# A GEGLU feed-forward in float32r: one H tile of each pair summed in its PSUM bank, and permuted rows moved from the output stores to the loads of layer norm 2

## The chip, the cores and the metric

One Trainium2 chip, one core. The metric is device microseconds of one execution. TensorE (PE) multiplies, VectorE (DVE), ScalarE (ACT) and GpSimd (POOL) do the rest; SyncE (SP) issues nearly all DMAs, ScalarE a few.

## The reference, cut

```python
h = x + attention(layernorm(x))              # 2048 tokens x 512, 32 heads, 4 segments of 512 tokens with a memory
g = layernorm(h) @ w_gate                    # 512 x 1376
u = layernorm(h) @ w_up
out = h + (gelu_tanh(g) * u) @ w_down        # 1376 x 512
```

All is float32. The kernel splits each operand of a product into a high and a low float32r part and adds three products (high x high, high x low, low x high).

## The kernel before

The tokens are 16 tiles of 128. The feed-forward treats them in two halves, `p` = 0 and 1, of two segments `s` of four tiles `t`. The 1376 columns are 11 blocks `f` (ten of 128, one of 96), taken in the order 0, 1, 10, 2, 3 to 9 (`forder`). What is written in the functions is only recorded: `pe`, `act`, `dve`, `pool` and `dma` make a list of steps, and the numbers of `ORDER` (lines 58 to 328) say in which order `Sched.run` issues them, each to its engine's own queue. `Val` stands for a buffer, which is handed out when its first step is issued; `row` buffers (128 x 512 floats), `slot`, `stk` and `stq` (a high and a low part) lie in SBUF, the eight `bank` in PSUM. Steps of one engine run in the order of its queue; SP's DMAs use eight completion semaphores in turn (DMAHW0 to DMAHW7, shared with the DMAs that ACT issues), and one waits until the one before it on its semaphore has landed.

`ffn(p, f, b)` (lines 1551 to 1613) multiplies weights and blocks of the normed tokens in seven products for a 2x2 block scheme, sums them (L1568 copies a bank, L1573 adds), and `geglu(s, g_, u_)` makes the H tile of block f and segment s: a square on ACT (L1579), a sum (L1581), a tanh on ACT (L1583), and two products on DVE (L1586, L1588). H tiles lie in `row` buffers as HH[p, f, s].

The down product takes pairs of blocks. For the first five pairs of half 0 and the first four of half 1 (`BY7`), `down7(p, n)` (lines 1704 to 1763) again makes seven products out of the four H tiles b11, b12 (block 2n) and b21, b22 (block 2n + 1). It needs t1 = b12 - b11, t2 = b22 - t1, t3 = b22 - b12 and t4 = b21 - t2 (`sub`, L1711 on DVE), and a `split` of the seven operands: a copy on ACT (L1716) and a difference on POOL, or on DVE for t2 and t4 of three pairs of half 0 (L1718). The products (L1737) are added into eight accumulators by DVE (L1748). `wd_prep` combines the weights of the pair for it.

At the end of a half, `turned(p)` transposes the accumulators (L716), stores them in pieces to y_dram, loads rows back (L1774), and adds on POOL the rows of g_dram, where the other blocks' sums were put (L1775). In half 0 that is the output, stored by L1778. In half 1 the pair of blocks 8 and 9 is still to come: `down(1, (8, 9), ..)` multiplies on TensorE (L1628), adds on DVE (L1636) and stores the output (L1641), the second half of the last tile by ACT's queue. `split` of its H tiles is L1593 on ACT and L1596 on POOL or DVE.

The normed tokens of half 1 are stored and loaded again by blocks (`swap`, t_dram), so that row 32 a + j of tile t is token 128 a + 32 t + j of its segment. `tokens(x, p, s, t)` gives these rows of a DRAM tensor: it is used for the loads of h for the first down sums (`acc`, L1799) and for the output stores.

Of the kernel before, what the change touches and what calls it, by code (L numbers as in the profile page):

```python
# [11 lines left out]
OP = mybir.AluOpType  # L12
# [3 lines left out]
P = 128  # L16
# [42 lines left out]
    6, 2, 10, 100, 0, 1, 4, 5, 11, 9, 7, 12, 13, 27, 14, 8, 16, 76, 77, 18, 91, 92, 93, 28, 29, 30, 15, 17, 88, 89,  # L59
    31, 32, 33, 44, 87, 23, 90, 34, 24, 46, 19, 20, 94, 95, 21, 22, 35, 36, 101, 37, 102, 103, 96, 822, 104, 25, 110,  # L60
    105, 42, 43, 38, 39, 40, 41, 821, 825, 97, 98, 99, 826, 827, 26, 828, 111, 106, 112, 628, 629, 107, 113, 108, 829,
    114, 109, 118, 48, 115, 50, 3, 52, 79, 119, 128, 129, 116, 117, 120, 164, 47, 133, 165, 121, 144, 51, 82, 167,
    168, 169, 145, 135, 146, 134, 147, 45, 139, 824, 130, 123, 124, 49, 53, 138, 81, 830, 54, 55, 831, 75, 131, 132,
    136, 58, 137, 140, 122, 186, 166, 189, 151, 149, 150, 148, 181, 184, 183, 185, 253, 254, 59, 74, 127, 190, 188,
    182, 57, 126, 187, 176, 178, 1024, 255, 823, 56, 173, 179, 175, 256, 125, 257, 180, 174, 177, 832, 833, 834, 60,
    61, 634, 1028, 835, 836, 67, 68, 258, 170, 171, 62, 172, 191, 192, 65, 66, 63, 64, 69, 70, 71, 259, 260, 72, 73,
    143, 142, 141, 197, 199, 162, 161, 198, 193, 194, 195, 196, 261, 270, 272, 271, 157, 277, 262, 263, 78, 266, 265,
    275, 152, 153, 264, 85, 273, 154, 837, 438, 439, 213, 216, 274, 217, 214, 215, 276, 440, 631, 224, 225, 226, 86,
    227, 228, 441, 278, 442, 239, 242, 243, 240, 1029, 203, 206, 205, 207, 234, 237, 443, 83, 238, 241, 235, 280, 268,
    1026, 204, 208, 209, 210, 211, 84, 163, 444, 229, 230, 279, 231, 212, 232, 233, 236, 200, 445, 245, 248, 838, 246,  # L70
    247, 201, 202, 218, 219, 446, 448, 449, 1027, 447, 839, 302, 303, 306, 450, 297, 299, 249, 244, 840, 80, 300, 632,
    220, 222, 221, 301, 1030, 298, 223, 304, 1414, 633, 281, 282, 841, 305, 155, 156, 842, 630, 250, 251, 283, 292,
    295, 294, 293, 1031, 406, 843, 296, 286, 287, 407, 635, 636, 328, 331, 332, 408, 844, 288, 845, 318, 329, 319,
    846, 847, 848, 320, 409, 410, 849, 321, 289, 313, 290, 291, 307, 308, 330, 269, 267, 366, 369, 368, 370, 314, 315,
    316, 317, 411, 323, 326, 324, 361, 365, 367, 364, 363, 362, 322, 412, 309, 413, 1025, 1032, 353, 355, 354, 158,
    625, 310, 311, 312, 626, 627, 414, 427, 429, 325, 334, 335, 336, 337, 797, 428, 433, 432, 356, 358, 357, 360, 437,
    434, 359, 798, 799, 430, 431, 415, 416, 421, 377, 380, 1033, 387, 388, 390, 800, 420, 801, 1034, 350, 352, 351,
    327, 333, 417, 378, 418, 338, 159, 1035, 284, 419, 391, 371, 339, 160, 340, 285, 372, 373, 374, 375, 392, 395,
    802, 382, 393, 394, 383, 384, 803, 398, 385, 386, 422, 482, 486, 485, 483, 804, 399, 1036, 466, 468, 401, 805,
    808, 484, 467, 807, 806, 809, 852, 586, 402, 477, 480, 1037, 481, 478, 381, 587, 376, 479, 503, 506, 379, 504,  # L80
    389, 514, 423, 588, 507, 396, 517, 469, 470, 515, 851, 505, 589, 472, 473, 518, 498, 499, 500, 501, 502, 590,
    1038, 1039, 397, 493, 496, 471, 474, 475, 508, 341, 511, 509, 591, 426, 476, 494, 424, 603, 425, 1417, 435, 436,
    541, 544, 542, 818, 252, 815, 592, 1040, 543, 819, 536, 538, 537, 545, 593, 539, 487, 488, 516, 489, 490, 491,
    492, 594, 595, 546, 540, 550, 596, 601, 608, 609, 610, 457, 600, 602, 458, 549, 1041, 512, 495, 510, 597, 598,
    497, 513, 547, 548, 400, 403, 404, 611, 612, 599, 519, 520, 1224, 578, 579, 580, 581, 582, 1225, 533, 535, 534,
    567, 568, 570, 571, 569, 613, 1226, 530, 532, 562, 563, 565, 531, 551, 552, 1227, 1228, 572, 614, 575, 573, 574,
    615, 662, 664, 663, 521, 617, 1042, 657, 658, 659, 405, 660, 661, 1229, 564, 604, 553, 554, 555, 1230, 649, 650,
    651, 666, 342, 665, 1231, 816, 1043, 557, 558, 559, 560, 1232, 616, 561, 566, 576, 652, 654, 656, 767, 1235, 1236,
    1418, 653, 820, 655, 556, 694, 697, 695, 1233, 344, 768, 646, 648, 647, 667, 1234, 618, 605, 606, 607, 781, 769,
    678, 681, 679, 770, 1044, 722, 771, 723, 726, 724, 343, 459, 460, 683, 686, 684, 850, 577, 583, 584, 785, 688,  # L90
    689, 1045, 1046, 1047, 1048, 1049, 685, 696, 817, 698, 725, 668, 1050, 1051, 691, 692, 1052, 772, 673, 522, 727,
    731, 729, 728, 674, 690, 773, 680, 682, 669, 730, 671, 670, 675, 676, 677, 687, 774, 672, 714, 715, 716, 775, 786,
# [1787 lines left out]
```

## Time and profile before

| | us |
|---|---|
| median of 3 runs (785.12 to 785.21) | 785.21 |
| the profiled execution | 783.71 |
| its span | 782.0 |
| TensorE busy | 726.2 |
| VectorE busy | 648.4 |
| ScalarE busy | 534.3 |
| GpSimd busy | 554.0 |

The granted TensorE clock is 0.983 of full on average. The profiled execution is 1.5 us under the median and 1.7 above its span. Start times count from the start of the span. A row of the timeline gives start, duration, engine, line, operation and tiles; a row of waits gives who waited, for whom, the sum in us, the count, the longest. "SPq" and "ACTq" are the queues that issue DMAs, and the duration there is that of the issue.

### The profile page before, as it was taken

The numbers are of one execution on the slowest core, as the hardware profiler recorded it, in microseconds if no ns is written. First come the engines' busy times: TensorE is split into PE (matmuls) and PEld (weight loads), VectorE is DVE, ScalarE is ACT, GpSimd is POOL, SyncE is SP. The second block draws the span as 40 slices with busy tenths as digits, with TensorE's granted clock in tenths as the row PEclk, the third lists the DMA queues.
The fourth block names the chain that finished last, engine by engine and source line by source line (L and its number), as shares of the span: only waits on it lengthen the run. The fifth ranks groups of instructions, "written<-read, shape, count | busy, mean of one in ns | idle before, by whom it ended". The sixth has DMA issues, their size and how long they took to land.

```text
span 782.0 us, 19221 instructions
## 1 busy us (share of the span) xinstructions
PE 726.2 (93%) x6442; PEld 569.7 (73%) x6442; DVE 648.4 (83%) x1978; ACT 534.3 (68%) x1138; POOL 554.0 (71%) x827
## 2 busy tenths in 40 slices
PE   7999999999999999999999998999999989999940
PEld 6877877777787776766777876787777768877830
DVE  7897989889887888999985667899999977889950
ACT  6879889796858778688675666787767746643500
POOL 6364342554745556888978999999999759999640
PEclk9999999999999999999999999999999999999985
DMA  6555556556567776767557466735752467665742
GB/s 242 135 154 145 136 151 188 140 162 175 157 181 180 227 200 167 220 202 189 179 157 229 136 233 188 226 126 150 219 170 102 113 200 230 208 230 184 190 122 81
DMA packets 100210, 137.32 MB, mean 176 GB/s; under 512 B 17440, under 2 KB 40144, under 8 KB 100112
## 3 DMA queue, kind: packets, MB, share of 16 engines
q1 hardware_dynamic: 99820, 135.71, 59.5%
q8 instruction: 51, 0.84, 0.5%
q10 hardware_dynamic: 292, 0.39, 0.2%
q14 instruction: 47, 0.39, 0.2%
HBM read 70.67 MB, written 39.26 MB: 141 GB/s over the span
## 4 chain that ended last, share of the span: by engine, by line
PE 22%; DVE 13%; POOL 10%; DMA 5%; issue 4%; ACT 2%; SPq 1%; POOLq 0%; DVEq 0%; ACTq 0%
PE bank L1561 12%; PE bank L1737 4%; DVE row L1748 2%; DVE row L1711 2%; POOL slot L1718 2%; POOL row L1533 2%; DMA g_dram<-row 2%; PE bank L1377 2%; PE bank L1297 1%; POOL half L1687 1%; POOL stq L1526 1%; POOL row L1775 1%; DVE bank L1573 1%; DVE row L1581 1%; POOL slot L1526 1%
## 5 line engine op out<-in xcount | busy, mean ns | idle before, releaser
L1275 ACT ACTIVATE row<-bank 128x512 f32<-128x512 f32 x320 | 171.8, 608 | 27.3 <-PE bank L1269 25.7
L1283 POOL TENSOR_SCALAR_AFFINE_SELECT row<-row 128x256 f32<-128x256 f32 (+1 forms) x320 | 108.7, 365 | 91.6 <-ACT row L1275 90.6
L1221 DVE CUSTOM_DVE_ANT_0 aside<-bank,amask 128x256 f32<-128x256 f32 (+2 forms) x384 | 141.0, 419 | 15.4 <-PE bank L1211 11.0
L957 PE MATMUL bank<-slot,slot 64*128 64x512 f32 x720 | 112.5, 404 | 0.1
L1561 PE MATMUL bank<-slot,slot 128*128 128x512 f32 (+1 forms) x354 | 95.2, 392 | 0.7 <-ACT vaug L1568 0.7
L1221 DVE CUSTOM_DVE_ANT_0 bank<-bank,amask 128x512 f32<-128x512 f32 x128 | 86.2, 710 | 8.6 <-PE bank L1211 7.8
L1269 PE MATMUL bank<-stq,stk 64*128 64x128 f32 (+3 forms) x512 | 81.7, 337 | 1.6 <-DVE bank L767 0.4
L1211 PE MATMUL bank<-stk,stq 64*128 64x512 f32 (+3 forms) x512 | 77.2, 329 | 4.0 <-DVE nm L1221 1.5
L1748 DVE TENSOR_TENSOR row<-row,bank 128x512 f32<-128x512 f32 x110 | 71.5, 675 | 10.8 <-PE bank L1737 9.4
L1297 PE MATMUL bank<-row,vaug 128*32 128x256 f32 (+3 forms) x1024 | 78.1, 436 | 1.1 <-DVE nm L1221 0.6
L1561 PEld LDWEIGHTS bank<-slot,slot 128*128 128x128 f32 (+1 forms) x354 | 65.4, 186 | 17.0 <-ACT vaug L1568 1.5
L957 PEld LDWEIGHTS bank<-slot,slot 64*128 64x128 f32 x720 | 70.8, 185 | 5.9 <-DVE tock L562 0.4
L1526 POOL TENSOR_TENSOR slot<-row,slot 128x512 fp32r<-128x512 f32 (+3 forms) x56 | 65.6, 1176 | 6.3 <-ACT slot L1524 5.7
L1211 PEld LDWEIGHTS bank<-stk,stq 64*128 64x128 f32 x512 | 53.3, 185 | 17.5 <-DVE nm L1221 2.8
L1269 PEld LDWEIGHTS bank<-stq,stk 64*128 64x128 f32 x512 | 55.3, 185 | 13.3 <-DVE nm L1221 3.5
L1737 PE MATMUL bank<-slot,half 128*128 128x512 f32 x216 | 58.2, 393 | 3.5 <-DVE row L1748 3.3
L1297 PEld LDWEIGHTS bank<-row,vaug 128*32 128x32 f32 x1024 | 29.8, 109 | 38.5 <-issue 32.9
L1006 PE MATMUL bank<-slot,slot 64*128 64x256 f32 x672 | 52.9, 284 | 0.0
L1561 PE MATMUL bank<-slot,stq 128*128 128x512 f32 (+1 forms) x180 | 50.5, 393 | 1.8 <-POOL stq L1526 1.2
L1737 PEld LDWEIGHTS bank<-slot,half 128*128 128x128 f32 x216 | 40.0, 188 | 14.0 <-DVE row L1748 5.6
L1221 DVE DVE_READ_ACCUMULATOR2_ANT nm<- 128x1 f32 x512 | 50.0, 98 | 0.0
L1006 PEld LDWEIGHTS bank<-slot,slot 64*128 64x128 f32 x672 | 47.5, 186 | 1.4 <-DVE z L1170 0.4
(225 smaller groups left out, 1779.0 us busy)
## 6 DMA issues: line engine op xcount, KB each, us to landing
stq<-slot SPq DMA_DIRECT2D x96, 128.0 KB
stk<-slot SPq DMA_DIRECT2D x94, 128.0 KB
row<-x SPq DMA_DIRECT2D x32, 256.0 KB
pv_dram<-row SPq DMA_DIRECT2D x32, 256.0 KB
row<-r_dram SPq DMA_DIRECT2D x28, 256.0 KB
wd_dram<-half SPq DMA_DIRECT2D x28, 256.0 KB
half<-wd_dram SPq DMA_DIRECT2D x28, 256.0 KB
row<-h_dram SPq DMA_DIRECT2D x24, 256.0 KB
```

What stands on the lines that cost most here:

```text
L957: return nc.tensor.matmul(pm[i].t, w[i].t[rows_of(r), wi, dc * P:(dc + 1) * P], XT[s][dc].t[rows_of(r), xi, :], start=(dc, wi, xi, ph) == ...
L1006: return nc.tensor.matmul(pms[n].t[:, 256 * t:256 * t + 256], XT[s][dc].t[rows_of(r), xi, t0:t0 + P], whl[wi].t[rows_of(r), dc // 2, 256 * ...
L1211: nc.tensor.matmul(sa.t[:, c0:c0 + w], sq.t[own, p, i * P:(i + 1) * P], sk.t[own, p, 0:w], start=True, stop=True, tile_position=(64 * a, 0 ...
L1221: nc.vector.tensor_tensor_reduce(out=(sa.t[:, c0:c0 + w] if i > 2 else aside[:, turns[0]:turns[0] + w]), in0=sa.t[:, c0:c0 + w], in1=amask ...
L1269: nc.tensor.matmul(sc.t[:, c0:c0 + D - q0], sk.t[own, p, q0:q0 + P], sq.t[own, p, q0:D], start=True, stop=True, tile_position=(64 * a, 0), ...
L1275: act(w, prio, lambda sc=sc, e=e: nc.scalar.activation(e.t[:, :w], sc.t[:, :w], AF.Exp), [sc, vtab], [e])
L1283: nc.gpsimd.affine_select(v, v, pattern=pat + [[1, P]], compare_op=OP.is_ge, fill=0.0, base=0, channel_multiplier=-1)
L1297: nc.tensor.matmul(pv.t[32 * n:32 * n + 32, kb * P:D], va.t[:, 136 * kb + 17 * j:136 * kb + 17 * j + 32], e.t[:, lo:lo + D - kb * P], star ...
L1526: pool(0.14 + 2.13e-3 * (hi - lo), prio, lambda: nc.gpsimd.tensor_tensor(v.t[:, 1, :hi - lo], r.t[:, lo:hi], v.t[:, 0, :hi - lo].bitcast(F ...
L1561: nc.tensor.matmul(dst.t[:w], v.t[:, wi, c0 + j * w:c0 + (j + 1) * w], b[bk][j].t[:, xi, :], start=first and j == 0 and n == 0, stop=j == ...
L1737: nc.tensor.matmul(dst[u].t, ws[a].t[0][:, wi, P * u:P * u + P], h[bk].t[:, xi], start=first and m == 0, stop=m == 2, skip_group_check=True)
L1748: dve(D, prio, lambda u=u, acc=acc: nc.vector.tensor_tensor(acc.t, acc.t, src[u].t, op=OP.add), [src[u]], [acc])
```

## The change

In `geglu` the last product of segment 1 of the odd block of a pair is written over the bank of g (`o = g_`), and this bank is HH[p, f, 1]. `down7` takes the odd block as b11, b12, so that b12 is the tile in the bank (`wd_prep` swaps the weights to fit); t3 is made first into a row, then t1 and after it t2 in the bank, then t4 into a row. The splits of t1 and t2 read the bank and are made by ACT and DVE, the other five of all pairs by ACT and POOL. `tokens` gives plain rows in both halves. Layer norm 2 of half 1 loads its rows in the permuted order instead, each tile by four loads of 32 rows, and its blocks are then in the plain order. ORDER is new throughout (2 lines of it longer).

```diff
-    6, 2, 10, 100, 0, 1, 4, 5, 11, 9, 7, 12, 13, 27, 14, 8, 16, 76, 77, 18, 91, 92, 93, 28, 29, 30, 15, 17, 88, 89,
...
+    5282, 5283,
@@ -1585,9 +1587,10 @@
             r = g_ if s else e
             dve(D, prio, lambda: nc.vector.scalar_tensor_tensor(
                 r.t[:w], e.t[:w], 1.0, g_.t[:w], op0=OP.add, op1=OP.mult), [g_, e], [r])
+            o = g_ if s and f % 2 and by7(p, f) else e
             dve(D, prio, lambda: nc.vector.scalar_tensor_tensor(
-                e.t[:w], r.t[:w], 0.5, u_.t[:w], op0=OP.mult, op1=OP.mult), [u_, r], [e])
-            HH[p, f, s] = hh or e
+                o.t[:w], r.t[:w], 0.5, u_.t[:w], op0=OP.mult, op1=OP.mult), [u_] if o is r else [u_, r], [o])
+            HH[p, f, s] = hh or o
             if not hh:
                 return
             act(D, prio, lambda: nc.scalar.activation(hh.t[:w, 0], e.t[:w], AF.Copy), [e], [hh],
@@ -1643,10 +1646,7 @@
 
     def tokens(x, p, s, t, cs=slice(0, D)):
         r0 = (8 * p + 4 * s) * P
-        if p == 0:
-            return x[r0 + t * P:r0 + t * P + P, cs]
-        return bass.AP(tensor=x.tensor, offset=x.offset + (r0 + 32 * t) * D + cs.start,
-                       ap=[[P * D, 4], [D, 32], [1, cs.stop - cs.start]])
+        return x[r0 + t * P:r0 + t * P + P, cs]
 
     vhalf = Val()
 
@@ -1665,7 +1665,7 @@
     def wd_prep(n):
         prio = at(0, 2 * n) - 12
         raw = [Val(PRAW), Val(PRAW)]
-        for r, f in zip(raw, (2 * n, 2 * n + 1)):
+        for r, f in zip(raw, (2 * n + 1, 2 * n)):
             dma(prio, lambda r=r, f=f: nc.sync.dma_start(r.t, wdp[f * P:f * P + P]), [], [r])
 
         def half(v, k):
@@ -1704,30 +1704,30 @@
     def down7(p, n):
         prio = at(p, 2 * n + 1) + 0.9
         ws = WDV[p, n]
-        b11, b12, b21, b22 = [HH[p, 2 * n + i, s] for i in range(2) for s in range(2)]
-        t1, t2 = Val(PC), Val(PC)
+        (b11, b12), (b21, b22) = [[HH[p, 2 * n + i, s] for s in range(2)] for i in (1, 0)]
+        t3, t4 = Val(PC), Val(PC)
 
         def sub(d, a, c):
             dve(D, prio, lambda: nc.vector.tensor_tensor(d.t, a.t, c.t, op=OP.subtract),
                 [v for v in (a, c) if v is not d], [d])
 
-        def split(v, on=pool):
-            hh = Val(PHH)
-            act(D, prio, lambda: nc.scalar.activation(hh.t[:, 0], v.t, AF.Copy), [v], [hh], src=0.09)
-            eng = nc.gpsimd if on is pool else nc.vector
-            on(1.23 if on is pool else D, prio, lambda: eng.tensor_tensor(
+        def split(v):
+            hh, psum = Val(PHH), v is b12
+            act(D, prio, lambda: nc.scalar.activation(hh.t[:, 0], v.t, AF.Copy), [v], [hh], src=0.067 if psum else 0.09)
+            eng = nc.vector if psum else nc.gpsimd
+            (dve if psum else pool)(D if psum else 1.23, prio, lambda: eng.tensor_tensor(
                 hh.t[:, 1], v.t, hh.t[:, 0].bitcast(F32), op=OP.subtract), [v], [hh])
             return hh
-        sub(t1, b12, b11)
-        h = {"11": split(b11), "t1": split(t1)}
-        sub(t2, b22, t1)
-        h["t2"] = split(t2, dve if p == 0 and n < 3 else pool)
-        h["21"] = split(b21)
+        h = {"11": split(b11), "21": split(b21)}
+        sub(t3, b22, b12)
+        sub(b12, b12, b11)
+        h["t1"] = split(b12)
+        h["t3"] = split(t3)
         sub(b12, b22, b12)
-        h["t3"] = split(b12)
+        h["t2"] = split(b12)
         h["22"] = split(b22)
-        sub(t2, b21, t2)
-        h["t4"] = split(t2, dve if p == 0 and n < 3 else pool)
+        sub(t4, b21, b12)
+        h["t4"] = split(t4)
         X, Y, Z = [[Val(PD) for _ in range(2)] for _ in range(3)]
 
         def prod(a, bk, dst, first=False):
@@ -1797,7 +1797,7 @@
             s, t = divmod(i, 4)
             n = 8 * p + 4 * s
             dma(at(p, 0) - 2 + i / 4, lambda i=i, s=s, t=t: nc.sync.dma_start(
-                a[i].t, tokens(h_dram, p, s, t)), HD[n:n + 4] if p else [HD[n + t]], [a[i]])
+                a[i].t, tokens(h_dram, p, s, t)), [HD[n + t]], [a[i]])
         return a
     halves()
     for p in range(2):
@@ -1815,9 +1815,11 @@
                     prio = at(0, 8) + s
                     rows = [Val(PROW2 if s else PROW) for _ in range(4)]
                     for t in range(4):
-                        r0 = (8 + 4 * s + t) * P
-                        dma(prio - 8, lambda t=t, r0=r0, rows=rows: nc.sync.dma_start(
-                            rows[t].t, h_dram[r0:r0 + P]), [HD[8 + 4 * s + t]], [rows[t]])
+                        for a in range(4):
+                            r0 = (8 + 4 * s + a) * P + 32 * t
+                            dma(prio - 8, lambda t=t, r0=r0, rows=rows, a=a: nc.sync.dma_start(
+                                rows[t].t[32 * a:32 * a + 32], h_dram[r0:r0 + 32]),
+                                [HD[8 + 4 * s + a]], [rows[t]], kb=70, dur=0.5, chain=True)
                     ln2(B[1], rows, s, prio, True, PD, swap=t_dram[s])
             if k < 22:
                 ffn_weights(*todo[k])
```

VectorE at a pair of half 1 (blocks 4 and 5). Before, with sums and differences in rows:

```order
L1586 SCALAR_TENSOR_TENSOR bank_66<-row_130,bank_66 128x512
L1588 SCALAR_TENSOR_TENSOR row_130<-bank_66,vaug_144 128x512
L1711 TENSOR_TENSOR row_118<-row_130,row_112 128x512
L1588 SCALAR_TENSOR_TENSOR row_133<-row_133,bank_65 128x512
L1748 TENSOR_TENSOR row_104<-row_104,bank_68 128x512
L1573 TENSOR_TENSOR bank_69<-vaug_142,bank_69 128x512
L1748 TENSOR_TENSOR row_115<-row_115,bank_66 128x512
L1711 TENSOR_TENSOR row_130<-row_113,row_130 128x512
L1711 TENSOR_TENSOR row_125<-row_113,row_118 128x512
```

and now (L1588 and L1591 are the products of `geglu`):

```order
L1591 SCALAR_TENSOR_TENSOR bank_67<-bank_67,vaug_145 128x512
L1711 TENSOR_TENSOR row_128<-row_115,bank_67 128x512
L1711 TENSOR_TENSOR bank_67<-bank_67,row_119 128x512
L1748 TENSOR_TENSOR row_124<-row_124,bank_66 128x512
L1718 TENSOR_TENSOR stq_98<-bank_67,stq_98 128x512
L1711 TENSOR_TENSOR bank_67<-row_115,bank_67 128x512
L1575 TENSOR_TENSOR bank_65<-vaug_141,bank_65 128x512
L1748 TENSOR_TENSOR row_114<-row_114,bank_70 128x512
L1711 TENSOR_TENSOR row_119<-row_107,bank_67 128x512
L1588 SCALAR_TENSOR_TENSOR row_131<-row_131,bank_68 128x512
L1583 SCALAR_TENSOR_TENSOR row_133<-row_133,bank_65 128x512
L1575 TENSOR_TENSOR bank_69<-vaug_142,bank_69 128x512
```

Where t1 (row_118 before), t2 and t3 were made from rows, bank_67 now holds the H tile, then t1, then t2, from the first row shown to the split of t2 that follows the last one shown.

SP at the end of the program. Before:

```order
L1774 DMA row_113<-y_dram 128x512 [waits DMAHW5_49]
L1778 DMA out_dram<-row_119 128x512 [waits DMAHW6_49]
L1774 DMA row_111<-y_dram 128x512 [waits DMAHW7_49]
L1774 DMA row_123<-y_dram 128x512 [waits DMAHW4_49,DMAHW2_49,DMAHW0_49]
L1774 DMA row_109<-y_dram 128x512 [waits DMAHW1_49]
L1774 DMA row_120<-y_dram 128x512 [waits DMAHW3_49]
L1641 DMA out_dram<-row_130 4x32x512 [waits DVE_49]
L1641 DMA out_dram<-row_121 4x32x256 [waits DVE_49]
L1778 DMA out_dram<-row_114 128x512 [waits DMAHW5_49,Pool_49]
L1641 DMA out_dram<-row_105 4x32x512 [waits DMAHW6_49,DVE_49]
L1641 DMA out_dram<-row_126 4x32x512 [waits DMAHW7_49,DVE_49]
L1641 DMA out_dram<-row_107 4x32x512 [waits DMAHW0_49,DVE_49]
```

and now (L1644 is the output store):

```order
L1774 DMA row_107<-y_dram 128x512 [waits DMAHW7_49,DMAHW2_49,DMAHW1_49]
L1774 DMA row_130<-y_dram 128x512
L1774 DMA row_129<-y_dram 128x512 [waits DMAHW3_49]
L1644 DMA out_dram<-row_123 128x512 [waits DVE_49]
L1644 DMA out_dram<-row_115 128x256 [waits DMAHW4_49,DVE_49]
L1644 DMA out_dram<-row_108 128x512 [waits DMAHW5_49,DVE_49]
L1778 DMA out_dram<-row_102 128x512 [waits DMAHW6_49]
L1644 DMA out_dram<-row_106 128x512 [waits DMAHW7_49]
L1644 DMA out_dram<-row_105 128x512 [waits DMAHW0_49,DVE_49]
L1644 DMA out_dram<-row_119 128x512 [waits DMAHW1_49,DVE_49]
L1644 DMA out_dram<-row_132 128x512 [waits DMAHW2_49,DVE_49]
L1644 DMA out_dram<-row_133 128x512 [waits DMAHW3_49,DVE_49]
```

Before, a store of half 0 that waits for DMAHW6, the semaphore of ACT's store (next fence), stood ahead of the last four loads from y_dram; now all loads stand ahead of the stores of L1644, these are plain, and the semaphore of ACT's store, DMAHW1, is next waited for by the third store from the end.

ACT at the end of the program. Before:

```order
L1579 ACTIVATE row_115<-bank_72 128x512 [waits DVE_49]
L1583 ACTIVATE row_115<-row_115 128x512 [waits DVE_49]
L1593 ACTIVATE slot_82<-row_131 128x512 [waits DVE_49]
L1593 ACTIVATE slot_75<-row_115 128x512 [waits DVE_49]
L1641 DMA out_dram<-row_108 4x32x256 [waits DMAHW6_49,DVE_49]
```

and now (L1596 splits an H tile, L1585 is the tanh):

```order
L1596 ACTIVATE slot_89<-row_124 128x512 [waits DVE_49]
L1596 ACTIVATE slot_78<-row_122 128x512 [waits DVE_49]
L1585 ACTIVATE row_127<-row_127 128x512 [waits DVE_49]
L1644 DMA out_dram<-row_112 128x256 [waits DMAHW1_49,DVE_49]
L1596 ACTIVATE slot_73<-row_127 128x512 [waits Activation_49]
```

ACT's store was its last instruction; now the copy of row_127 into slot_73 stands behind it.

538 rows, old and new, of the table ORDER are left out of this document.

## The prediction

> **What bounds the kernel now.** I read the page's first part, then the engines' busy time by stage, then the end of the timeline, and from there the waits, the chain and the groups by shape.
>
> ```profile
> PE 726.2 (93%) x6442; PEld 569.7 (73%) x6442; DVE 648.4 (83%) x1978; ACT 534.3 (68%) x1138; POOL 554.0 (71%) x827
> ```
>
> TensorE is busy for 726.2 of 782.0 us; the change leaves every matmul in place. So only the other 55.8 us can move. Some 29 of them lie behind the last matmul, as the timeline shows; the rest are holes. In the feed-forward stage, by windows (columns: PE, weight loads, DVE, ACT, POOL, clock, DMA share, GB/s):
>
> ```profile
> 450.00:500.00 50.00, 46.96 (x203) 37.48 (x202) 37.62 (x58) 30.95 (x66) 49.45 (x50) 1.00 0.68 215
> 500.00:550.00 50.00, 48.81 (x210) 38.64 (x210) 46.98 (x112) 40.95 (x83) 49.13 (x50) 1.00 0.50 153
> 550.00:600.00 50.00, 47.62 (x203) 36.84 (x202) 48.80 (x88) 35.10 (x71) 49.13 (x52) 1.00 0.61 182
> 600.00:650.00 50.00, 46.33 (x200) 35.85 (x199) 41.69 (x87) 29.27 (x56) 36.73 (x37) 1.00 0.48 142
> 650.00:700.00 50.00, 49.89 (x221) 40.96 (x219) 41.81 (x59) 29.76 (x56) 48.94 (x44) 1.00 0.68 218
> ```
>
> PE's holes here are 3.0, 1.2, 2.4, 3.7 and 0.1 us, 10.4 in all. GpSimd is full from 450 to 600, VectorE nearly so from 500; from 650 TensorE sets the pace. The end of the timeline:
>
> ```profile
> 722.54 0.98 SPq L720 DMA_DIRECT2D y_dram<-row  x2
> ...
> 741.88 0.43 SPq L1774 DMA_DIRECT2D row<-y_dram  x1
> ...
> 748.64 1.14 ACTq L1641 DMA_DIRECT2D out_dram<-row  x1
> ...
> 751.72 1.52 PE L1628 MATMUL bank<-stq,slot 128*128 128x512 f32 x6
> 752.03 0.36 SPq L1778 DMA_DIRECT2D out_dram<-row  x1
> 752.43 1.87 SPq L1774 DMA_DIRECT2D row<-y_dram  x4
> 755.46 4.93 POOL L1775 TENSOR_TENSOR row<-row,row 128x512 f32<-128x512 f32 x4 [8.38 <-DMA out_dram<-row]
> 757.47 10.73 SPq L1641 DMA_DIRECT2D out_dram<-row  x6
> 760.43 0.69 DVE L1636 TENSOR_TENSOR row<-row,bank 128x512 f32<-128x512 f32 x1 [0.54 <-POOL row L1775]
> ```
>
> The last matmul ends at 753.2, the last VectorE sum at 761.1, the span at 782.0. From the second to the third, 20.9 us, only output stores run. How wide they run (same columns):
>
> ```profile
> 760.00:765.00 5.00, 0.00 (x0) 0.00 (x0) 0.69 (x1) 0.00 (x0) 0.40 (x1) 0.50 0.25 74
> 765.00:770.00 5.00, 0.00 (x0) 0.00 (x0) 0.00 (x0) 0.00 (x0) 0.00 (x0) 0.50 0.26 100
> ```
>
> A share of 0.25 to 0.26 is four DMA engines of 16, each moving 25 GB/s. These stores are the form 4x32x512, whose slowest dimension is 4. While plain 256 KB transfers run, the share is far higher:
>
> ```profile
> 585.00:590.00 5.00, 5.00 (x23) 3.89 (x22) 4.84 (x9) 1.96 (x5) 5.00 (x5) 1.00 0.92 313
> 725.00:730.00 5.00, 5.00 (x24) 4.14 (x23) 4.73 (x16) 2.29 (x4) 4.40 (x4) 1.00 0.88 209
> ```
>
> Waits of the issuing queues, and three transfers from the chain (start, duration):
>
> ```profile
> SPq L1876 <- DMA out_dram<-row: 12.7, 1, 12.7
> SPq L1778 <- DMA out_dram<-row: 9.7, 1, 9.7
> ```
> ```profile
> 496.21 4.42 DMA g_dram<-row
> ...
> 627.28 8.12 DMA g_dram<-row
> ...
> 748.64 3.38 DMA out_dram<-row
> ```
>
> SP stood from 742.3 to 752.0 until ACT's half store had landed: the DMAs share eight semaphores in turn, and SP's next one used the same. Four y_dram loads stood behind that DMA, and so the last four adds on GpSimd and six sums on VectorE.
>
> **The change, term by term.** The profiled execution took 783.71 us, 1.7 more than its span; the median of the three runs shown, 785.21, is 1.5 above it.
>
> *Stores of half 1 become plain 128x512.* Before, last sum to end: 20.9. After: issue 0.4 and landing. The bounds of a landing are 3.4 (a half store into empty queues) and 8.1 (a store behind four-engine loads). I take 4.4, the plain 256 KB store nearest to the case, and 0.8 for a store ahead of it (256 KB at 313 GB/s): 5.5 in all. Gain 15.4; ends 12.8 and 17.5.
>
> *The place of the ACT store.* In the new order the y_dram loads stand on SP ahead of every store of lines L1644, and only the third store from the end shares a semaphore with ACT's. So the last sum follows the last matmul by some 1.0 (0.69 and a start) in place of 7.9: gain 6.9.
>
> *But ACT's store now stands ahead of an ACT split* (slot_73 <- row_127) for which the last 15 matmuls of TensorE wait. That is a new wait. SP made 39 issues from 722.54 to 742.31, 0.51 each. In the new order 36 lie from the first y_dram store to the load of row_114; the first store stands 26.6 us of matmul work ahead of the end (28.9 before, which in the trace was 30.7). So the load issues about 10 us ahead of the end, lands 3 later, then an add (1.3, with one add before it), two half sums (0.8), the issue (1.1), and the split 0.6 with a start of 0.5: TensorE can begin 1.9 before its old end, where 3.4 us of work stand. I take a loss of 2; ends 0 and 4.
>
> *Loads of half 1 for the first down sums* (row<-h_dram, 4x32 before, plain now):
>
> ```profile
> DVE row L1636 <- DMA row<-h_dram: 3.2, 1, 3.2
> PE bank L1628 <- DVE row L1636: 2.2, 2, 1.2
> PE bank L1737 <- DVE row L1748: 3.3, 3, 1.9
> ```
>
> The second row is TensorE's share of that wait, from 630 to 638; the 8.1 us store is from there too. Gain 2.2; ends 0 and 3.7, the hole of that window.
>
> *Sums in the bank.* Groups by shape (count | busy, mean ns):
>
> ```profile
> L1711 DVE TENSOR_TENSOR row<-row,row 128x512 f32<-128x512 f32 x36 | 41.1, 1153 | 1.6 <-DMA h_dram<-row 0.8 <-DMA g_dram<-row 0.4
> L1718 DVE TENSOR_TENSOR slot<-row,slot 128x512 fp32r<-128x512 f32 x5 | 5.6, 1125 | 0.8 <-ACT slot L1716 0.8
> L1718 POOL TENSOR_TENSOR slot<-row,slot 128x512 fp32r<-128x512 f32 x31 | 42.3, 1367 | 1.4 <-ACT slot L1716 1.4
> L1748 DVE TENSOR_TENSOR row<-row,bank 128x512 f32<-128x512 f32 x110 | 71.5, 675 | 10.8 <-PE bank L1737 9.4 <-issue 1.1
> L1422 DVE TENSOR_TENSOR slot<-bank,slot 128x512 fp32r<-128x512 f32 x5 | 3.4, 688 | 1.5 <-ACT slot L1417 1.5
> ```
>
> ```profile
> L1711 DVE TENSOR_TENSOR row<-row,row x36: 650/1086/3214, 436.3 to 714.1; 128x512 f32<-128x512 f32 x36
> ```
>
> A VectorE difference with both inputs in SBUF takes 1.15 on average and 0.65 at the least (the last row: least, median, most), so nearly half of it is waiting inside the instruction; with one input in PSUM it takes 0.68. [...] All 36 differences get an operand in PSUM: 36 x (1.153 - 0.675) = 17.2 less on VectorE. Its splits go from 6 (5.6 and 0.7) to 18 of 0.688 = 12.4: 6.1 more. VectorE gains 11.1 net. GpSimd loses 12 splits x 1.367 = 16.4, four in half 0 and eight in half 1, and is held up less. ACT makes the same copies, 18 of them from a bank: nothing. This is off the path except where TensorE waited: the holes other than the 2.2 are 8.2. I take half, 4; ends 0 and 8.
>
> [...]
>
> *The price.* The bank of one H tile is held until the split of t2, and the differences run in a row: t1 needs the last H tile, t2 overwrites t1 and so waits for both engines that split it. Before, t1 and both of its splits could be made after the first f tile. TensorE has seven banks meanwhile. No row shows it; below lies 0 (other products stand between), above 1.9 in each of nine pairs, the longest wait of L1737 quoted: 17. Since the order puts products of other tiles between the splits, it is nearest to 0: I take 1.
>
> *Loads of layer norm 2.* Eight become 32 of 64 KB, and a row now needs all four tiles of its segment. Before (least, median, most ns of an issue; first and last start):
>
> ```profile
> L1388 SPq DMA_DIRECT2D h_dram<-row x16: 320/424/583, 329.8 to 475.5; - x16
> L1819 SPq DMA_DIRECT2D row<-h_dram x8: 319/344/887, 417.0 to 516.0; - x8
> ```
>
> 24 issues more x 0.51 = 12 us of SP's time. In the new order the last of them stands 222 us of matmul work ahead of the end and half 1's first product 169, so 53 us of other products hide them: cost 0. Without that cover it would be up to 12.
>
> Sum: 782.0 - 15.4 - 6.9 + 2 - 2.2 - 4 + 1 = 756.5. With 1.7 the execution, with 1.5 the median: 759.7.
>
> **Rivals.**
> 1. *Slower: the held bank.* Each pair's serial differences keep L1737 waiting. For it: the longer sequence. Against: 1.9 is the longest wait of its kind and the bank is one of eight. The gains without the price are 26.5, so it decides from 3.0 us a pair; at 3.3 it gives 759.7 - 1 + 29.7 = 788.
> 2. *The 32 narrow loads hold SP*, so weights behind them come late, and TensorE stands for most of the 12: 770. Against: y_dram's stores of 32 partitions fill the engines to 0.88 in the row above. [...]
> 3. *The change doesn't do what it says*: the stores are slow by the DRAM side, not by the form, and the 15.4 don't come: 775.
> 4. *The middle gives nothing*: holes of 8.2 stay, the bank costs half a us a pair more (4.5), and 2.2 stay: 759.7 + 4 + 4.5 + 2.2 = 770. For it: all of the order is new, also in attention, where nothing else changes.
> 5. *The middle gives all*: holes gone, no loss at ACT's store: 759.7 - 4 - 1 - 2 = 753.
>
> **How the numbers follow.** Forecast 0.55, its own range 755 to 765; rivals 0.04, 0.08, 0.05, 0.16 and 0.12 in turn. The range 751 to 770 holds the forecast, 5, and most of 2 and 4; it leaves out 1, 3 and what lies above 770. A change of 0.2% (1.6 us) is about what can be told from none. Faster 0.96, same 0.01, slower 0.03: only rival 1 is not faster.
>
> **What would show it.** After: no window at the end with a share near 0.25 for more than 2 us; the last sum within 2 us of the last matmul and the end within 8 of it; L1711 at about 0.68; GpSimd's L1718 at 45; SP without a wait near 9.7; a TensorE wait of 1 to 3 us for ACT near the end. Wrong would be: stores as plain 128x512 that still fill a quarter of the engines, or waits of L1737 and L1561 that sum to over 20 us from 450 on.

## The result and the profile after

The changed kernel takes 740.3 us (median of four runs, 739.54 to 744.56) against 785.16 for the kernel before in the same session: ratio 0.944, 95% interval 0.941 to 0.948. The forecast was 759.7 with a range of 751 to 770, so the time lies 10.7 below the range. The gain was 45 us, not 25.

The page's first part, the profiled execution of 740.42 with a span of 738.7:

```profile
PE 719.6 (97%) x6442; PEld 570.6 (77%) x6442; DVE 634.8 (86%) x1990; ACT 534.0 (72%) x1138; POOL 523.1 (71%) x815
```

The same windows of the middle as before, and two at the end (PE, weight loads, DVE, ACT, POOL, clock, DMA share, GB/s):

```profile
450.00:500.00 50.00, 50.00 (x221) 41.08 (x221) 38.05 (x88) 38.62 (x84) 47.58 (x51) 1.00 0.73 231
500.00:550.00 50.00, 50.00 (x222) 41.41 (x221) 48.66 (x109) 42.35 (x87) 46.83 (x52) 1.00 0.69 204
550.00:600.00 50.00, 49.53 (x215) 38.76 (x213) 48.88 (x98) 33.43 (x66) 45.66 (x52) 1.00 0.37 108
600.00:650.00 50.00, 50.00 (x221) 40.88 (x220) 42.15 (x74) 32.71 (x63) 35.55 (x35) 1.00 0.81 246
650.00:700.00 50.00, 50.00 (x223) 41.34 (x222) 45.78 (x74) 27.08 (x50) 42.01 (x40) 1.00 0.61 192
720.00:730.00 10.00, 9.69 (x49) 7.84 (x47) 8.17 (x13) 3.23 (x6) 8.89 (x8) 1.00 0.89 277
730.00:739.00 9.00, 3.25 (x13) 2.36 (x13) 4.11 (x7) 0.00 (x0) 2.67 (x2) 0.97 0.56 208
```

Read the numbers in brackets, not only the busy time. TensorE makes 221 matmuls in 50 us when nothing holds it, as from 650 to 700 before. Before, the other four windows had 203, 210, 203 and 200. Now all five have 215 to 223. A matmul then takes 50 / 221 = 0.226. GpSimd is still busy for 46 to 48 of 50 us up to 600 and VectorE for 49 from 500 to 600; they no longer hold TensorE.

The end of the timeline:

```profile
727.79 0.38 ACTq L1644 DMA_DIRECT2D out_dram<-row  x1
728.22 0.63 ACT L1596 ACTIVATE slot<-row 128x512 fp32r<-128x512 f32 x1 [4.13 <-DVE row L1639]
...
730.32 3.25 PE L1631 MATMUL bank<-stq,slot 128*128 128x512 f32 x13 [0.63 <-DVE slot L1599]
...
732.32 2.05 DVE L1639 TENSOR_TENSOR row<-row,bank 128x512 f32<-128x512 f32 x3 [0.26 <-PE bank L1631]
732.35 2.91 SPq L1644 DMA_DIRECT2D out_dram<-row  x5
```

The last matmul ends at 733.57, the last sum at 734.37, the span at 738.7. What lies behind the last matmul fell from 28.8 to 5.1 us, 23.7 less. The last matmul itself comes 19.7 earlier, and that is where the forecast was far off. The groups of the differences and splits:

```profile
L1711 DVE TENSOR_TENSOR row<-row,bank 128x512 f32<-128x512 f32 x18 | 12.3, 681 | 1.6 <-ACT slot L1716 1.0 <-ACT stk L1716 0.3
L1718 DVE TENSOR_TENSOR slot<-bank,slot 128x512 fp32r<-128x512 f32 x15 | 10.2, 683 | 0.8 <-ACT slot L1716 0.7
L1718 POOL TENSOR_TENSOR slot<-row,slot 128x512 fp32r<-128x512 f32 x24 | 30.9, 1297 | 3.1 <-ACT slot L1716 3.1
L1718 POOL TENSOR_TENSOR stq<-row,stq 128x512 fp32r<-128x512 f32 x9 | 11.7, 1299 | 3.3 <-ACT stq L1716 3.3
```

GpSimd's splits into `slot` and `stq` take 1.30 each, where they took 1.37 and 1.46 before (those into `stk` took 1.30 in both): two engines got faster, not one. The last two groups before:

```profile
L1718 POOL TENSOR_TENSOR stq<-row,stq 128x512 fp32r<-128x512 f32 x16 | 23.4, 1463 | 0.4 <-ACT stq L1716 0.4
L1718 POOL TENSOR_TENSOR stk<-row,stk 128x512 fp32r<-128x512 f32 x10 | 13.0, 1298 | 2.1 <-ACT stk L1716 2.1
```

### The profile page after: what moved, and what is told of

It is laid out like the page before. It is cut to its first block, busy times and chain, and to the rows that moved or that the text cites. A ratio compares the mean times of both kernels' runs of the same rounds, so it can differ in the third digit from the quotient of the medians.

```text
span 738.7 us, 19243 instructions
## 1 busy us (share of the span) xinstructions
PE 719.6 (97%) x6442; PEld 570.6 (77%) x6442; DVE 634.8 (86%) x1990; ACT 534.0 (72%) x1138; POOL 523.1 (71%) x815
## 4 chain that ended last, share of the span: by engine, by line
PE 67%; DVE 11%; issue 3%; POOL 2%; DMA 2%; ACT 2%; SPq 1%; ACTq 0%; DVEq 0%; POOLq 0%
PE bank L1563 23%; PE bank L959 8%; PE bank L1299 7%; PE bank L1737 7%; PE bank L1271 5%; PE bank L1213 4%; PE bank L1379 3%; PE bank L1372 3%; PE bank L1008 3%; DVE row L1748 2%; DVE aside L1223 2%; PE bank L1631 2%; DVE bank L1223 1%; PE bank L1181 1%; DMA t_dram<-row 1%
## 5 line engine op out<-in xcount | busy, mean ns | idle before, releaser
L1563 PE MATMUL bank<-slot,slot 128*128 128x512 f32 (+1 forms) x366 | 97.3, 390 | 0.0
L1299 PE MATMUL bank<-row,vaug 128*32 128x512 f32 (+3 forms) x1024 | 79.0, 436 | 1.8 <-DVE nm L1223 1.2
L1213 PE MATMUL bank<-stk,stq 64*128 64x256 f32 (+3 forms) x512 | 78.9, 326 | 1.7 <-DVE nm L1223 1.1
L1563 PEld LDWEIGHTS bank<-slot,slot 128*128 128x128 f32 (+1 forms) x366 | 67.8, 186 | 15.8 <-ACT stq L1419 0.4
L959 PEld LDWEIGHTS bank<-slot,slot 64*128 64x128 f32 x720 | 73.3, 185 | 6.0 <-DVE nm L1223 0.7
L1528 POOL TENSOR_TENSOR slot<-row,slot 128x512 fp32r<-128x512 f32 (+3 forms) x60 | 67.1, 1124 | 14.1 <-ACT slot L1526 14.0
L1213 PEld LDWEIGHTS bank<-stk,stq 64*128 64x128 f32 x512 | 56.1, 185 | 9.6 <-DVE nm L1223 2.4
L1737 PE MATMUL bank<-slot,half 128*128 128x512 f32 x234 | 61.7, 390 | 0.0
L1570 ACT ACTIVATE vaug<-bank 128x512 f32<-128x512 f32 (+1 forms) x66 | 38.5, 591 | 18.6 <-PE bank L1563 18.5
L1737 PEld LDWEIGHTS bank<-slot,half 128*128 128x128 f32 x234 | 43.8, 188 | 9.6 <-DVE row L1748 0.4
L1008 PEld LDWEIGHTS bank<-slot,slot 64*128 64x128 f32 x672 | 48.7, 186 | 1.0 <-DVE mb L1138 0.2
```

The costliest lines, as they stand in the source:

```text
L959: return nc.tensor.matmul(pm[i].t, w[i].t[rows_of(r), wi, dc * P:(dc + 1) * P], XT[s][dc].t[rows_of(r), xi, :], start=(dc, wi, xi, ph) == ...
L1008: return nc.tensor.matmul(pms[n].t[:, 256 * t:256 * t + 256], XT[s][dc].t[rows_of(r), xi, t0:t0 + P], whl[wi].t[rows_of(r), dc // 2, 256 * ...
L1213: nc.tensor.matmul(sa.t[:, c0:c0 + w], sq.t[own, p, i * P:(i + 1) * P], sk.t[own, p, 0:w], start=True, stop=True, tile_position=(64 * a, 0 ...
L1299: nc.tensor.matmul(pv.t[32 * n:32 * n + 32, kb * P:D], va.t[:, 136 * kb + 17 * j:136 * kb + 17 * j + 32], e.t[:, lo:lo + D - kb * P], star ...
L1528: pool(0.14 + 2.13e-3 * (hi - lo), prio, lambda: nc.gpsimd.tensor_tensor(v.t[:, 1, :hi - lo], r.t[:, lo:hi], v.t[:, 0, :hi - lo].bitcast(F ...
L1563: nc.tensor.matmul(dst.t[:w], v.t[:, wi, c0 + j * w:c0 + (j + 1) * w], b[bk][j].t[:, xi, :], start=first and j == 0 and n == 0, stop=j == ...
```

## The experiments

All were timed beside the kernel before, whose medians lie between 783.6 and 785.2 in the five sessions. So medians of different sessions are compared within about 1.6 us. The ratios are to the kernel before, with 95% intervals.

| kernel | median us | ratio, interval |
|---|---|---|
| t1, before with plain stores | 765.8 | 0.977 (0.975 to 0.979) |
| t2, and plain loads of h | 762.6 | 0.973 (0.971 to 0.976) |
| t3, before with the half store by SP | 779.8 | 0.994 (0.992 to 0.996) |
| f2, before with all three | 755.1 | 0.962 (0.959 to 0.966) |
| t4, after with 4x32x512 stores | 756.0 | 0.965 (0.963 to 0.967) |
| m1, after with the sums in rows | 763.7 | 0.973 (0.971 to 0.975) |
| m4, and those splits on GpSimd | 780.0 | 0.994 (0.992 to 0.996) |
| m10, after with twelve splits twice | 747.4 | 0.952 (0.949 to 0.955) |
| m5, before with half splits on GpSimd | 775.5 | 0.988 (0.984 to 0.991) |
| m8, before with half differences | 779.8 | 0.993 (0.990 to 0.996) |
| m11, f2 with about the change's relief | 751.6 | 0.958 (0.956 to 0.960) |
| m2, before with after's attention order | 793.3 | 1.012 (1.009 to 1.014) |
| m3, after with before's attention order | 749.6 | 0.954 (0.952 to 0.957) |
| f3, after with wide loads of layer norm 2 | 740.3 | 0.944 (0.942 to 0.946) |
| f4, after with the half store by SP | 738.7 | 0.942 (0.941 to 0.944) |

### The end: stores, loads, the half store

**t1.** In `tokens`:

```diff
-        if p == 0:
+        if p == 0 or x is out:
```

> The kernel before, in its own order, with the output stores of half 1 alone as plain 128x512 (L1641): the output's rows of half 1 then lie in permuted places, which the copy leaves so. Theory A (the form 4x32x512 keeps the stores on four DMA engines): last sum to end 20.9 becomes about 5.5, so 785.2 becomes 769.8 (767.7 to 772.4), and no window at the end stays near a DMA share of 0.25. Rival (the DRAM side sets the pace): 785, share still near 0.25.

784.3, the kernel before timed beside it, became 765.8, 18.5 less (by the ratio's interval 16 to 20), and 2 under the range of theory A. The last sum ends at 760.7, near the 761.1 of before, and the span 3.7 later in place of 20.9. The last window of its profile:

```profile
760.00:764.40 4.40, 0.00 (x0) 0.00 (x0) 0.69 (x1) 0.00 (x0) 0.01 (x1) 0.50 0.57 219
```

A share of 0.57 where 0.25 stood: the form kept the stores on four engines, and the DRAM side did not. Theory A holds in its mechanism. The term was 15.4; the span shows 17.2, since the landing took the lower bound of the forecast.

**t4.** The same form put back into the kernel after.

> The kernel after with the output stores of half 1 again as 4x32x512 (the rows of half 1 then lie in permuted places of the output). Theory A: the end behind the last sum grows from 4.4 to about 20, so 740.3 becomes 755.7 (753 to 758), with a DMA share near 0.25 at the end. Rival (in the new order the stores start earlier and the form costs little): 741 to 746.

756.0, 15.7 more than the kernel after. The share at the end is a quarter again:

```profile
740.00:750.00 10.00, 0.00 (x0) 0.00 (x0) 0.00 (x0) 0.00 (x0) 0.00 (x0) 0.50 0.26 93
```

**t2.** `if p == 0` becomes `if p in (0, 1)`, so the loads of L1799 are plain too.

> The copy of the kernel before with plain output stores, and the loads of h for the first down sums of half 1 (L1799) plain too: the rows added in half 1 are then other tokens' rows. Theory D (these loads, on four engines, hold the first down sums and TensorE from 630 to 638): 2.2 less than with plain stores alone (0 to 3.7), 767.6. Rival (the time is given back at the next wait): the same as with plain stores alone, within 0.5.

3.2 less than t1, so theory D holds, with 3.2 for 2.2 and inside its ends.

**t3.** One queue for both halves:

```diff
-                        n, q = 8 * p + 4 * s + t, nc.scalar if i else nc.sync
+                        n, q = 8 * p + 4 * s + t, nc.sync
```

> The kernel before with the second half store of the last tile issued by SP in place of ACT, which puts it in SP's queue behind the last four loads from y_dram; nothing else. Theory B (SP stood 9.7 us for the semaphore of ACT's store, and the last four loads, adds and sums behind it): last sum follows the last matmul by 1 to 2 in place of 7.9, so 785.2 becomes 779 (778 to 781). Rival (the stores on four engines are a queue of their own, and starting earlier only lengthens it): 783 to 785.

4.5 less (interval of the ratio 3 to 6), inside the range of theory B. The timeline:

```profile
751.07 5.15 DVE L1636 TENSOR_TENSOR row<-row,bank 128x512 f32<-128x512 f32 x8 [0.27 <-POOL row L1775]
...
754.11 12.34 SPq L1641 DMA_DIRECT2D out_dram<-row  x6
```

The wait went as forecast: the last sum ends 0.8 behind the last matmul (755.4) in place of 7.9. But the span ends 22.0 behind that sum, so the stores on four engines still took their time. TensorE ended 2.2 later than in the profile before; the clock of this profile is 0.97 in the windows from 0 to 50 and from 550 to 600, which is some 1.5 us lost in each, and the profile before has 1.00 up to its last matmul.

**f2.** t2 and t3 in one kernel, in the old order.

> The kernel before in its own order with all that the change does at the end and at the loads, and nothing in its middle: plain output stores and plain loads of h (the rows of half 1 then are other tokens' rows), the half store by SP. If the parts add up: 785 - 21.7 - 4.5 = 759 (757 to 761), and the 19 that then remain to 740.3 belong to the sums in the bank and the new order. If the end hides one part behind the other: 762 to 764, and the remainder is 22 or more.

755.1, 29.7 less than before and under both ranges. With plain stores the half store's place is worth 762.6 - 755.1 = 7.5, where it was 4.5 alone. By the traces, the last sum comes 1.3 behind the last matmul in place of 7.0 in t2, which is 5.7 of it; besides, the clock of t2's profile is 0.97 from 550 to 600 (some 1.5 us lost) and that of f2's 1.00. The last matmul ends at 747.5, the last sum at 748.8, the span at 752.2: the end of the kernel after, in the old order. So 14.8 us remain to 740.3, and nearly all lies ahead of the last matmul (747.5 against 733.6).

### The middle: the bank, the two engines, the order

**m1.** The kernel after with one line undone, in its own order but for two steps of VectorE and three of SP:

```diff
-            o = g_ if s and f % 2 and by7(p, f) else e
+            o = e
```

> The kernel after, in its order but for two steps of VectorE and three of SP, with the odd block's H tile of segment 1 in its row again (o = e), so that t1 and t2 are made in that row and all 36 differences and 18 splits on VectorE read SBUF alone. [...] Order theory (the new order hides it): 740 to 744.

763.7, 23.4 more than the kernel after and far above the order theory: the new order does not hide the sums in rows. Its groups, the largest wait of TensorE from 400 on, and three windows:

```profile
L1711 DVE TENSOR_TENSOR row<-row,row 128x512 f32<-128x512 f32 x36 | 40.5, 1125 | 3.1 <-DMA h_dram<-row 1.9 <-POOL stk L1528 0.6
L1718 DVE TENSOR_TENSOR slot<-row,slot 128x512 fp32r<-128x512 f32 x15 | 16.6, 1109 | 0.9 <-ACT slot L1716 0.7
L1716 ACT ACTIVATE slot<-row 128x512 fp32r<-128x512 f32 x39 | 24.4, 626 | 21.5 <-DVE row L1711 12.0 <-DVE row L1591 6.5 <-PE bank L1563 1.8
```
```profile
PE bank L1563 <- ACT vaug L1570: 6.1, 5, 2.3
```
```profile
552.50:555.00 2.50, 0.97 (x5) 0.45 (x3) 2.50 (x4) 1.33 (x3) 2.50 (x2) 1.00 0.78 206
555.00:557.50 2.50, 1.73 (x5) 1.40 (x6) 2.50 (x6) 2.50 (x6) 2.50 (x4) 0.75 0.81 230
557.50:560.00 2.50, 2.50 (x8) 1.96 (x8) 2.15 (x4) 2.50 (x6) 2.50 (x4) 0.57 0.80 208
```

Both forms are back at 1.1; ACT's copies wait 12.0 for the differences, and TensorE for ACT. The windows show a price that idle time does not: behind the hole the clock fell to about half, and 8 matmuls stand where 12 or 13 should. Three such drops cost 5.1 of the 23.4 (the clock's shortfall, summed over windows of 1 us).

**m4.** Sums in rows as in m1, and `psum = False`, so that GpSimd makes all 63 splits.

> As the kernel with the sums in rows, and the 18 splits of t1 and t2 on GpSimd too (63 in all, six more than the kernel before has). Bank theory: GpSimd, 97% busy from 425 to 575, gets 18 x 1.3 = 23 us more, which it cannot hide: 760 to 775. Order theory: up to 748.

780.0, above what was expected of the bank theory, and far above the order theory.

**m10.** VectorE as in the kernel after; GpSimd makes the splits of t3 and t4 of six pairs twice:

```diff
+            twice = v in (t3, t4) and (p == 1 or n >= 3)
...
-                hh.t[:, 1], v.t, hh.t[:, 0].bitcast(F32), op=OP.subtract), [v], [hh])
+                hh.t[:, 1], v.t, hh.t[:, 0].bitcast(F32), op=OP.subtract) for _ in range(1 + twice)], [v], [hh])
```

> The kernel after with GpSimd's splits of t3 and t4 of six pairs made twice over (same result), twelve more of 1.3, which gives GpSimd the 57 of before; VectorE keeps its sums in the bank. GpSimd theory (the twelve splits taken off GpSimd made the gain): 12 x 1.3 = 15.6 comes back nearly whole, 740.3 becomes 753 (749 to 757). VectorE theory: 740 to 744.

747.4, 7.1 more: less than half of the 15.6, and more than the VectorE theory allows. So GpSimd's load is a part of the gain and not all of it. TensorE now waits for GpSimd's splits (L1719 here):

```profile
PE bank L1738 <- POOL stk L1719: 1.8, 2, 0.9
PE bank L1738 <- POOL half L1687: 1.4, 1, 1.4
PE bank L1738 <- POOL stq L1719: 1.1, 1, 1.1
```

**m5 and m8.** The kernel before, with GpSimd's splits or VectorE's differences over half of the columns:

```diff
-                hh.t[:, 1], v.t, hh.t[:, 0].bitcast(F32), op=OP.subtract), [v], [hh])
+                hh.t[:, 1, :c], v.t[:, :c], hh.t[:, 0, :c].bitcast(F32), op=OP.subtract), [v], [hh])
```
```diff
-            dve(D, prio, lambda: nc.vector.tensor_tensor(d.t, a.t, c.t, op=OP.subtract),
+            dve(D, prio, lambda: nc.vector.tensor_tensor(d.t[:, :256], a.t[:, :256], c.t[:, :256], op=OP.subtract),
```

> The kernel before with GpSimd's differences of the splits (L1718, 57 of them) over 256 of 512 columns: half of the low parts is left as it was. GpSimd theory (99% busy from 450 to 600, it sets the pace of the middle): 57 x 0.65 = 37 us less on it, the middle loses its holes and the slack in its matmul counts, 15 in all: 770 (768 to 774). VectorE theory (differences from two SBUF rows, 1.15 each, set it): those wait half as long, 36 x 0.25 = 9 us less on VectorE: 777 to 781. Neither: 784.

> The kernel before with VectorE's 36 differences (L1711) over 256 of 512 columns: half of each sum is left out. VectorE theory: 1.15 becomes about 0.6, 20 us less on VectorE, a little more than the sums in the bank give: 770 to 774. GpSimd theory: 782 to 785.

m5 took 775.5 (9.3 less), m8 779.8 (5.0 less). Each lies between its two theories: neither engine alone set the pace. The differences, in m5 and then in m8:

```profile
L1711 DVE TENSOR_TENSOR row<-row,row 128x512 f32<-128x512 f32 x36 | 35.6, 999 | 1.8 <-DMA h_dram<-row 1.0 <-DMA g_dram<-row 0.4
```
```profile
L1711 DVE TENSOR_TENSOR row<-row,row 128x256 f32<-128x256 f32 x36 | 28.7, 807 | 1.7 <-POOL stq L1718 1.2
```

Half the columns saved 0.35 in m8, about half of the work alone (0.65 at the least); the other half microsecond is waiting and stays. With GpSimd's splits halved, in m5, the waiting shrank by 0.15. How such a wait looks at its worst, in m8 (VectorE, then GpSimd):

```profile
441.29 5.36 DVE L1718 TENSOR_TENSOR slot<-row,slot 128x512 fp32r<-128x512 f32 x1 [0.76 <-ACT slot L1716]
```
```profile
440.18 1.50 POOL L1596 TENSOR_TENSOR stk<-row,stk 96x512 fp32r<-96x512 f32 x1
441.65 1.29 POOL L1718 TENSOR_TENSOR slot<-row,slot 128x512 fp32r<-128x512 f32 x1
442.90 0.74 POOL L1687 TENSOR_TENSOR half<-row,half 128x256 fp32r<-128x256 f32 x1
443.60 1.28 POOL L1526 TENSOR_TENSOR slot<-row,slot 128x512 fp32r<-128x512 f32 x1
444.84 1.26 POOL L1526 TENSOR_TENSOR stq<-row,stq 128x512 fp32r<-128x512 f32 x1
446.07 1.18 POOL L1687 TENSOR_TENSOR half<-row,half 128x256 fp32r<-128x256 f32 x1
```

One VectorE split, 0.68 at the least in the kernel before, began while a GpSimd instruction ran and stood through the next four, which follow each other without a gap. It ended at 446.65, inside a GpSimd step of 1.18 whose form has a median of 0.74. TensorE then waited 2.2 for this split, and behind the wait the clock fell to half, which cost 1.7 more. Without these 3.9, m8 would be 8.9 under the kernel before, near m5; that is an estimate from these numbers.

**m11.** f2 with the differences over half the columns, and 24 of GpSimd's 57 splits too: about the relief of the change, in the old order.

> The kernel of 755.1 (before's order, plain stores and loads, half store by SP) with VectorE's 36 differences over 256 columns, and GpSimd's splits of t1 to t4 in six pairs (24 of 57) over 256 columns: half of those sums and low parts is left out. The work taken off, 36 x 0.35 = 13 on VectorE and 24 x 0.55 = 13 on GpSimd, is about what the change takes off. Relief theory: the middle's loss goes in the old order too, 755 becomes 743 (740 to 747). Order theory: 751 to 755, and the rest is the order's.

751.6, 3.5 less than f2, and inside the range of the order theory. But the same split of VectorE takes 5.35 here too, and behind it come:

```profile
PE bank L1738 <- DVE slot L1719: 2.2, 1, 2.2
```
```profile
450.00:454.00 4.00, 4.00 (x12) 3.14 (x12) 2.68 (x5) 1.58 (x4) 2.78 (x3) 0.57 0.50 171
```

The wait and the drop of the clock took 2.2 + 1.7 = 3.9 at one place. Without them the relief would be worth about 7.4, an estimate from these two numbers.

**m2 and m3.** The steps up to the first feed-forward product in the other kernel's order, spliced to the kernel's own order behind.

> The kernel before with the first 3086 steps in the order of the kernel after, up to the first feed-forward product, and from there in its own order (four steps moved for buffers). Order theory: the attention part ends earlier by what the cumulated matmul counts show at 450 us (35 matmuls of the feed-forward more, 8 us), and that carries to the end: 785.2 becomes 777 (774 to 781). Bank theory: the gain is made only where sums and differences run, so 784 to 786.

> The kernel after with its steps up to the first feed-forward product in the order of the kernel before, and from there in its own. Order theory: 740.3 becomes 748 (744 to 751). Bank theory: 740 to 742.

m3 took 749.6 (9.3 more than after), inside the range of its order theory. m2 took 793.3, which neither theory expected. At m2's seam TensorE waited for ACT, and the clock fell:

```profile
PE bank L1269 <- ACT row L1275: 6.1, 2, 5.8
```
```profile
385.00:390.00 5.00, 1.77 (x5) 1.06 (x5) 0.76 (x1) 2.09 (x4) 4.92 (x8) 0.50 0.18 54
390.00:395.00 5.00, 5.00 (x15) 3.40 (x14) 0.00 (x0) 2.66 (x5) 2.29 (x7) 0.52 0.00 0
```

The longest wait, 5.8, and 5.1 of lost clock make 10.9 of the seam's own; without it m2 would be 2.5 under the kernel before. m3's seam has this wait:

```profile
PE bank L1181 <- DVE tock L564: 2.1, 1, 2.1
```

With 5.1 of lost clock (1.7 of it at the program's start) that is 7.2; without it m3 would be 2.1 above the kernel after. So the attention's new order gives perhaps 2 or 3. That is an estimate, and counts bear it out: at 450 us the five profiles with the old order there and no edit ahead of it (before, t1, t2, t3, f2) have 1246 to 1258 matmuls left, the five with the new one (after, t4, m10, f4, and f3, whose loads alone lie there) 1233 to 1243. The means, 1252 and 1239, are 13 x 0.226 = 2.9 us apart.

### The two small terms

**f3.** The eight wide loads of layer norm 2 in the kernel after.

> The kernel after with the loads of layer norm 2 of half 1 again as eight of 128x512 in plain order, each at the place of the last of the four narrow ones (the rows of half 1 then reach the feed-forward unpermuted). The prediction's term (other work hides the 24 more issues, 0): 739.5 to 741. Rival (the narrow loads hold SP for up to 12): 730 to 737.

740.3, no change: the 24 more issues are hidden, as forecast.

**f4.** The edit of t3 in the kernel after.

> The kernel after with the second half store of the last tile issued by SP, so that nothing stands ahead of ACT's last split (slot_73). The prediction's term (TensorE waits 2 for that split): 738.3 (737 to 739). Rival (the split waits for VectorE's half sum anyway, since the trace gives TensorE only 0.63 of wait there): 739.5 to 741.

738.7, 1.6 less than the kernel after by the medians, and the lowest of all versions; the intervals of the two ratios overlap, and f3 of the same session lies at 740.3. The number is inside the term's range, but the trace speaks for the rival:

```profile
724.68 0.63 ACT L1596 ACTIVATE slot<-row 128x512 fp32r<-128x512 f32 x1 [2.32 <-DVE row L1591]
726.06 0.75 DVE L1639 TENSOR_TENSOR row<-row,bank 128x256 f32<-128x256 f32 x2 [0.88 <-POOL row L1775]
726.73 1.62 DVE L1599 TENSOR_TENSOR slot<-row,slot 128x512 fp32r<-128x512 f32 x1
728.41 3.24 PE L1631 MATMUL bank<-stq,slot 128*128 128x512 f32 x13 [0.48 <-DVE slot L1599]
```

ACT's copy now runs 3.5 earlier. But VectorE's half of the split still stands behind two half sums, which wait for GpSimd, and TensorE waits 0.48 for it in place of 0.63. The last matmul ends 1.9 earlier than in the profile of the kernel after; the group of 26 matmuls ahead of the wait begins 1.74 earlier already (722.50 against 724.24), and 7 fewer matmuls are left at 450 us, far ahead of the edit. So the trace gives the wait 0.2 at most.

## Why the prediction was wrong, step by step

| step | forecast | runs |
|---|---|---|
| stores plain | -15.4 | -18.5 (t1) |
| place of the half store and last sum | -6.9 | -7.5 (t2 to f2) |
| loads of h for the down sums | -2.2 | -3.2 (t1 to t2) |
| ACT's store ahead of ACT's split | +2 | 0.2 at most by the traces (f4; 1.6 by the medians) |
| loads of layer norm 2 | 0 | 0.0 (f3) |
| sums in the bank, held bank, new order | -4 + 1 | -14.8 (f2 to after) |

The three gains outside the middle had the right mechanisms: each run moved the way the term says, and their sizes were short by 4.7 together. The middle was short by 11.8, and the loss of 2 is not seen. These make 18.5 of the 19.4 between 759.7 and 740.3; the rest is the kernel before, which took 784.3 in place of 785.2 beside t1. What the profile was to show, it shows, but for one: no end window near 0.25, the last sum 0.8 behind the last matmul and the end 5.1 behind it, L1711 at 0.68, GpSimd's L1718 at 45, no wait of SP near 9.7. The new wait of TensorE is 0.63 and not 1 to 3, and it is for VectorE's half of the split. ACT's copy stood 4.13 behind the store, as forecast, but VectorE's queue would have held the split nearly as long (f4).

The step that failed is the size of the middle: "This is off the path except where TensorE waited: the holes other than the 2.2 are 8.2. I take half, 4". The runs show 14.8 there, for a net forecast of 3. These counts show where it lies (five windows of 50 us, in which a matmul on an edge counts twice):

| kernel | matmuls from 450 to 700 us | left at 450 us |
|---|---|---|
| before | 1037 | 1253 |
| f2 | 1049 | 1250 |
| m11 | 1074 | 1266 |
| m1 | 1019 | 1252 |
| m10 | 1075 | 1236 |
| m3 | 1102 | 1282 |
| after | 1102 | 1240 |

From f2 to the kernel after, 53 more matmuls in the middle are 12.0 us at 0.226 each, and 10 fewer left at 450 are 2.3, near the 13.9 by which the last matmul comes earlier. (At 450, m3's number holds the wait and the drop of its seam, and m1's and m11's their first pair, which begins ahead of 450.) The step failed in three ways.

- The holes were not the whole loss. From 450 to 700 the kernel before made 1037 matmuls and the kernel after 1102. The 65 are 14.7 us. The holes shrank from 10.4 to 0.5, which is 9.9; the other 4.8 stood inside "busy". All five rows lay in the prediction with their counts, and the counts were not read.
- Half of the holes was taken, and nearly all of them went. VectorE's stretched differences and GpSimd's long queue did not each have a slack of their own. A late difference makes a late copy on ACT, a late split and a late product: ACT's copies wait for the differences in m1, and TensorE waits for GpSimd's splits in m10. In the new order the bank alone is worth 23.4 (m1), twelve splits on GpSimd 7.1 (m10).
- The order was counted at nothing. Attention's part is the 2 to 3 ahead of 450. The middle does not need it: m3, with attention in the old order, makes the same 1102 matmuls there. The corners around the rest: old order without relief 755.1 (f2), old order with about the relief 751.6 (m11), new order with the sums in rows 763.7 (m1), new order with them in the bank 740.3. In the old order the relief gains 3.5; the new order with the sums in rows loses 8.6 against f2; order and bank together gain 14.8. So the two are worth more together than apart. The corners are not clean: m1 also has twelve splits on VectorE in place of GpSimd, and one place costs m11 3.9. How the 12.0 of the middle divides between the feed-forward's order and the relief is not settled; an order made anew for the sums in rows was not tried.

The held bank cost nothing that can be seen: TensorE's waits from 400 on are 0.6, 0.2 and 0.2 in all. Rival 5, "the middle gives all", went the right way, and its price was too small for the same reason as the step.

## What to carry to other kernels

Where TensorE sets the pace, compare counts of equal matmuls per window with the best window of the same stage; the difference is what a change can give at most, and idle time shows only part of it (9.9 of 14.7 here). In this kernel a VectorE difference with two SBUF inputs beside a full GpSimd took 1.15, and 0.65 at the least: the difference is waiting. An operand in PSUM brought it to 0.68, and GpSimd's slowest splits from 1.46 to 1.30. A new instruction order and the edit that it was made for are best priced as one thing: here the order with the sums in rows lost.

## What the runs showed that was not expected

- VectorE can be held up for far longer than one instruction: 5.36 us in m8 and 5.35 in m11 for a step of 0.68, while GpSimd stands busy without a gap. In m8 the VectorE step began at 441.29, inside a GpSimd instruction that had begun at 440.18, and so far the later one waited; but when the running GpSimd instruction ended, VectorE did not get in, and the next four GpSimd instructions went ahead of it. No run shows what decides which of the two goes first.
- A wait of TensorE of about 2 us can be followed by a drop of the clock to half, for about 3.4 us and a loss of 1.7 on top (in m8 the five windows of 1 us from 446 have 0.86, 0.50, 0.50, 0.50 and 0.93): so in m1 behind waits of 2.3 and 2.0, in m8 and m11 behind 2.2. In m3 the drop at the wait of 2.1 lasted twice as long and cost 3.4. In t1, t2 and t3 the clock is 0.97 in the window from 550 to 600, where TensorE has holes of 2.3, 2.1 and 2.3. But the kernel before and f2 have holes of 2.4 and 1.8 in that window, each with a wait of 1.9 near 550, and a clock of 1.00, and a wait of 2.4 in m2, at 649 us, has no drop behind it. So the length of the wait alone does not decide, and no run shows what does. In m4 one drop, at 387, has no wait above 0.5 ahead of it.
